# Retention and two gated layers on one core: the second table behind the first keys, side work up to unit 5 in another order, and a limit on the bytes of loads in flight

## The chip, the cores and the metric

One core of one Trainium2 chip runs the kernel. The metric is the device time of one execution in microseconds. The engines are called as in the profile: PE (TensorE matmul), PEld (its weight loads), DVE (VectorE), ACT (ScalarE), POOL (GpSimd) and SP (SyncE, which here only issues transfers). A "q" behind the name of an engine means the sequencer that issues its instructions and transfers.

## What is computed

The reference has three stages; the output of each is the input of the next.

```python
# q, k, v: (2, 8, 768, 64); scale = 1/8
for t in range(S):
    state = gamma * state + einsum('bhd,bhe->bhde', k[:, :, t], v[:, :, t])
    y[:, :, t] = scale * einsum('bhd,bhde->bhe', q[:, :, t], state)
x = y.transpose(0, 2, 1, 3).reshape(1536, 512)
x = (x @ w_a) * (x @ w_b) @ w_out             # 512 -> 1536 -> 512
h = x @ w_in                                  # 512 -> 2048
out = maximum(0.01 * h, h) @ w_out2           # 2048 -> 512
```

`gamma` is one constant for each of the 8 heads. All numbers are float32.

## The kernel before

**Units.** The first stage is cut into 12 units: three tiles of 512 tokens, and in each four pairs of heads. Unit u has four input tiles of 128x512 float32 (256 KB): queries `q`, keys turned `k`, keys plain `n`, values `v`. In the trace all units share these names, so that `q` at one time is the `q` of whichever unit stands there. For each unit the kernel makes scaled keys `kd` and scaled queries `qs`, the scores `sc` (PE), masked scores `P` (DVE), the products of keys and values `kv` (PE), running states (`cb` and `ca` in units 0 to 3, `cr` and `ca` from unit 4 on; DVE), and the output bank `x` (PE), which gets a part from `P` ("within") and a part from the states ("across"). Units 0 to 3 are "wide" (chunks of 128 tokens; their states are copied into the tile `wk` by ACT, `wide_spreads`); units 4 to 11 use chunks of 64 tokens.

**Splitting.** The large products are made of float32 numbers split in two: `x00h` is the high part of the output of tile 0, pair 0 and `x00l` the rest. ACT makes the high part (`x_high`), and the low part is made by DVE (`x_low`), or by POOL from the copy `xf` (`copy_x`). The weights come as raw words (`raw_a`, `raw_b`, 512 KB each), which ACT and DVE round in six steps (`begin_steps` on ACT, tiles `a` and `sl`; `round_steps` on DVE, min, shift and add) before they are split as well (`a0h`, `a0l`).

**Order.** The schedule is written out by hand: each engine executes its instructions in the order of the program, and waits where an operand is not there yet. One loop over u issues for each step the scores and states of unit u + 1 and the output of unit u. From unit 4 on the loop also puts pieces of the first dense layer between (`fill`, generator `first_blocks`): the first piece is the bank `pa`, whose twelve matmuls (L1016) read `x00h`, `x00l`, `x01h`, `x01l`, `x02h`, `x02l`, `x03h`, `x03l` with `a0h`, and then four of them with `a0l`. In the rest of the kernel, two dense layers, PE works through a list of matmuls.

**Transfers.** Two small tables hold constants: `table` (74 KB) is needed for the first scaled queries and keys, `rest` (198 KB) holds among others the causal mask of the first `P`, the rows from which POOL makes `grown`, and the factors of `kd4` and later. ACT issues both. SP issues all inputs, first the four tiles of units 0 to 3, then of unit 4, then `raw_a0`, unit 5, `raw_b0`, unit 6, and so on. Each transfer uses one of eight completion semaphores in turn, so an issue waits until the transfer eight places before it has landed.

**Before the first unit** PE runs ten matmuls on a tile `warm` that DVE has cleared.

Of the kernel before, what the change touches and what calls it, by code (L numbers as in the profile page):

```python
# [9 lines left out]
F32 = mybir.dt.float32  # L10
F32R = mybir.dt.float32r
F16 = mybir.dt.float16
BF16 = mybir.dt.bfloat16
# [7 lines left out]
P = 128  # L21
# [14 lines left out]
NRAW = 4  # L36
NEXTRA = 10
NWARM = 10
FILL = {4: 4, 5: 6, 6: 6, 7: 6, 8: 6, 9: 6, 10: 6, 11: 4}
PUMP = {7: 1.2, 8: 1.6, 9: 1.2, 10: 1.2, 11: 1.2}  # L40
ROUND = {3: ("a", 0, 3), 4: ("b", 0, 3), 5: ("a", 1, 3), 6: ("b", 1, 3)}
# [188 lines left out]
def retention_moe_kernel(ctx: ExitStack, tc: tile.TileContext, ins, out):  # L230
# [11 lines left out]
    def bank(name):  # L242
        return psum.tile([P, TT], F32, tag="ps", name=name)
# [32 lines left out]
    first_layer = len(order)  # L276
    order += second
    source = {"a": (wab, 0), "b": (wab, 1), "wo": (wo, 0), "wi": (w2, 0), "wq": (w2, 1)}
    raws, begun, rounded, dram = {}, {}, {}, {}
    at = {"load": 0, "begin": 0, "round": 0, "queued": 0, "hold": True}  # L280

    def wait_for(later, done):
# [2 lines left out]
            mybir.DependencyInfo(mybir.DependencyClass.Sync, mybir.DependencyReason.DATA),  # L285
        )

    def load_weights(behind=()):
        if at["load"] < len(order) and at["load"] < at["round"] + NRAW:
            kind, f = order[at["load"]]  # L290
            src, i = source[kind]
            t = rawp.tile([P, TT], I64, tag="raw", name=f"raw_{kind}{f}")
            load = nc.sync.dma_start(t, src[f, i])
            if behind:
                wait_for(load, behind[-1])
            raws[kind, f] = t
            at["load"] += 1
# [11 lines left out]
    def begin_steps():  # L309

        n = at["begin"]
        key = order[n]
        raw = raws[key]
        u = slots.new(F32, f"{key[0]}{key[1]}")
        sl = tmp.tile([P, TT], I32, tag="sl", name=f"sl{n}")
        nc.scalar.activation(u, word(raw, F32, 1), AF.Abs, scale=2.0 ** -112)
        yield
        nc.scalar.mul(half(sl, F16, 1), word(raw, F32, 1), 2.0 ** -100)
        yield
        nc.scalar.mul(half(sl, U16, 0), word(raw, U32, 0), 2.0 ** -29)  # L320
        begun[key] = (u, sl)
        at["begin"] += 1
# [191 lines left out]
        return t.rearrange("p (m t) -> p m t", m=SUB)  # L514

    def known(f):
        return lambda u: f(u, *units[u], un[u]) if 0 <= u < len(units) else []

    def loads(u):
        if u >= len(units):  # L520
            return
        d = un[u] = {}
        source = {"q": qT, "k": kT, "n": kn, "v": vn}
        for name in "qknv" if u < NPAIR else "nvqk":
            d[name] = slots.new(F32, f"{name}{u}")
            nc.sync.dma_start(d[name], source[name][units[u]])

    flip = heads[::-1]
    cols = [slice(j * P, (j + 1) * P) for j in range(CPT)]
# [68 lines left out]
        slots.done(1)  # L598

    @known  # L600
    def scaled_keys(u, t, p, d):
        d["kd"] = slots.new(F32, f"kd{u}")
        nc.scalar.activation(d["kd"], d["n"], AF.Copy, scale=small[:, p:p + 1])

    @known
    def scaled_queries(u, t, p, d):
# [71 lines left out]
    @known  # L678
    def masked(u, t, p, d):
        d["P"] = slots.new(F32, f"P{u}")  # L680
        n = 2 * NPAIR + p
        pace[:] = nc.vector.scalar_tensor_tensor(
            by_sub(d["P"]), by_sub(d["sc"]), small[:, n:n + 1], within_sub, op0=ALU.mult, op1=ALU.mult
        ),
# [16 lines left out]
    @known  # L701
    def copy_x(u, n, p, d):
        t = TURN[n]
        if t != 1:
            xf[t, p] = slots.new(F32, f"xf{t}{p}")
            if t:
                nc.scalar.mul(xf[t, p], d["x"], -1.0)
            else:
                nc.scalar.copy(xf[t, p], d["x"])
            if u < NPAIR - 2:  # L710
                nc.gpsimd.tensor_sub(x[t, p][1], xf[t, p], as32(x[t, p][0]))
        slots.done(6)
        del un[u]
# [246 lines left out]
            leave(0, 1, [m], u["p1"], nc.vector.tensor_add, z.acc["p3"])  # L960


    warm = ap.tile([P, TT], BF16, tag="warm", name="warm")
    nc.vector.memset(warm, 0.0)
    nc.scalar.dma_start(table, head)
    loads(0)
    nc.scalar.copy(carry[0][0][:, 0:1], warm[:, 1:2])
    nc.scalar.dma_start(rest, more)
    grow_tables()
    wps = bank("warm")  # L970

    def keep_warm(n):
        for _ in range(n):
            nc.tensor.matmul(wps, warm[:, 0:P], warm, start=True, stop=True)

    keep_warm(NWARM)
    for u in range(1, 4):
# [59 lines left out]
    def keys(u):  # L1037
        (wide_keys if u < NPAIR else scaled_keys)(u)
# [28 lines left out]
    for u in range(-1, len(units)):  # L1067
        if u < NPAIR:
            if u < NPAIR - 1:
                wide_scores(u + 1)  # L1070
            else:
                wide_within(u)
                issue(states(u + 1))
                issue(scores(u + 1))
            if u < 0:
                queries(1)
                keep_warm(3)
            if u < NPAIR - 1:
                wide_states(u + 1)
            else:  # L1080
                un[u + 1]["copy"]()
                for step in un[u + 1]["adds"][:2]:
                    step()
                masked(u + 1)
                for step in un[u + 1]["adds"][2:]:
                    step()
                for _ in rounds:
                    pass
            if u < 0:
                wide_within(0)  # L1090
            if 1 < u < NPAIR - 1:
                wide_within(u)
            wide_across(u)
            if not u:
                wide_within(1)
            if u == NPAIR - 2:
                keys(NPAIR)
                queries(NPAIR)
            x_high(u)
            if u == NPAIR - 2:  # L1100
                begin = begin_steps()
                next(begin)
                wide_spreads(u + 1)
                keys(NPAIR + 1)
                queries(NPAIR + 1)
                for _ in begin:
                    pass
                x_low(u)
                rounds = weigh_steps(u + 1)
                next(rounds)  # L1110
                next(rounds)
                loads(u + AHEAD)
                slots.tick()
                continue
            if u < NPAIR - 1:
                wide_spreads(u + 1)
            if u < 0:
                keys(1)
            for v in KEYS.get(u, ()):
                keys(v)  # L1120
                queries(v)
            if u == NPAIR - 1:
                copy_x(u - 1)
                high(done.pop())
                x_low(u)
                low()
                keys(NPAIR + 2)
                begin_weights()
            copy_x(u)
            slots.tick()  # L1130
        else:
            issue(states(u + 1), within(u))
            issue(scores(u + 1), across(u))
            slots.tick()
            steps = un[u + 1]["adds"] if u + 1 in un else []
            mid = len(steps) // 2
            if steps and u > NPAIR:
                un[u + 1]["copy"]()
            if u == NPAIR:
                masked(u + 1)  # L1140
                un[u + 1]["copy"]()
                for step in steps:
                    step()
                x_high(u)
                queries(u + 2)
                weigh(u)
                high(done.pop())
                x_low(u)
                low()
                begin_weights()  # L1150
            else:
                low()
                for step in steps[:mid]:
                    step()
                masked(u + 1)
                for step in steps[mid:mid + 1]:
                    step()
                keys(u + 2)
                for v in QUERIES.get(u, ()):
                    queries(v)  # L1160
                leave_x(u)
                for step in steps[mid + 1:]:
                    step()
                if u == NPAIR + 1:
                    fill(u)
                rounding(u)
            copy_x(u)
        if u != NPAIR + 1:
            fill(u)
        pump(PUMP.get(u, 0))  # L1170
        loads(u + AHEAD)
        if u < 0:
            load_weights()
        if u in (5, 6, 8, 9, 10, 11):
            load_weights(pace if u > 6 else ())
        if u == 9:
            at["hold"] = False
        if u == 6:
            enqueue_next(2)
            queue.extend(behind)  # L1180
            behind.clear()
            queue.extend(sub_items(("a", 2), ("b", 2)))
        if u == 8:
            for d, a in outer:
                nc.gpsimd.dma_start(xf[d], xf[a], accum_op=ALU.add)
        if u == 8:
            spare.extend(mixed_items(xf, S, "s", True))
        for _ in range(min(LATER.get(u, 0), len(spare))):
            spare.pop(0)[1]()
        slots.tick()  # L1190
# [438 lines left out]
```

## Time and profile before

| | us |
|---|---|
| median of 3 runs | 557.0 (556.24 to 559.15) |
| profiled execution, whole | 557.07 |
| its span, first to last instruction | 555.3 |
| PE busy in the span | 548.9 (99%) |
| DVE busy | 457.5 (82%) |
| ACT busy | 385.8 (69%) |
| POOL busy | 158.9 (29%) |

The table is read from the top: 1.77 us of the profiled execution lie outside the span. PE is busy nearly all the time; matmuls are pipelined and their ends are modelled, so that the idle 6.4 us are not all that PE could save. Nearly all of the trace in which PE is not the engine that sets the pace lies in the first 45 us, in which the inputs are loaded.

### The profile page before, as it was taken

What the parts mean: (1) busy time and instruction counts of PE and PEld (TensorE: products, weight loads), DVE (VectorE), ACT (ScalarE), POOL (GpSimd) and SP (SyncE); (2) the same over time, 40 slices, a digit from 0 to 9 for tenths busy, and PEclk for the clock granted to TensorE, in tenths of its full rate; (3) what the DMA queues carried; (4) which work ended last, traced back from release to release, by engine and by line L of the source; (5) the groups of instructions that cost most, each with busy time, mean ns of one, the idle gap of its engine ahead of it and who ended that gap; (6) DMA issues with size and microseconds to landing.
All of it is one profiled execution on the core that took longest, in us unless ns stands there. A gap on an engine that the chain in (4) does not pass through costs nothing.

```text
span 555.3 us, 10484 instructions
## 1 busy us (share of the span) xinstructions
PE 548.9 (99%) x3743; PEld 462.5 (83%) x3743; DVE 457.5 (82%) x973; ACT 385.8 (69%) x797; POOL 158.9 (29%) x203
## 2 busy tenths in 40 slices
PE   8999999999999999999999999999999999999997
PEld 5878888888888888888888888888888888888886
DVE  4877967889898898899789859896977798999862
ACT  4867377877789888867758457769766886687800
POOL 3524201113231430267520320221433556700000
PEclk9999999999999999999999999999999999999999
DMA  8996934548788987899992362665787799964111
GB/s 313 393 375 167 217 93 119 154 133 212 195 253 219 259 220 253 260 305 240 243 186 94 66 125 71 184 181 158 231 240 233 206 272 242 223 164 118 58 58 57
DMA packets 49765, 108.19 MB, mean 195 GB/s; under 512 B 5936, under 2 KB 13360, under 8 KB 49712
## 3 DMA queue, kind: packets, MB, share of 16 engines
q1 hardware_dynamic: 27360, 66.60, 36.7%
q0 software_dynamic: 22064, 40.64, 34.5%
q8 instruction: 29, 0.48, 0.3%
q10 hardware_dynamic: 288, 0.28, 0.2%
q14 instruction: 24, 0.20, 0.1%
HBM read 73.68 MB, written 18.35 MB: 166 GB/s over the span
## 4 chain that ended last, share of the span: by engine, by line
PE 95%; DMA 3%; DVE 1%; issue 0%; ACT 0%; SPq 0%
PE blk L258 12%; PE blk L257 12%; PE blk L259 12%; PE top L257 6%; PE top L258 5%; PE top L259 5%; PE pa L257 4%; PE pa L259 4%; PE pa L258 4%; PE pb L257 4%; PE pb L259 4%; PE pb L258 4%; PE mid L257 3%; PE mid L259 3%; PE mid L258 3%; DMA q<-in_qT 2%
## 5 line engine op out<-in xcount | busy, mean ns | idle before, releaser
L258 PE MATMUL blk<-form,form 128*128 128x512 f32 (+1 forms) x224 | 75.8, 339 | 0.0
L257 PE MATMUL blk<-form,form 128*128 128x512 f32 (+1 forms) x224 | 75.6, 337 | 0.0
L259 PE MATMUL blk<-form,form 128*128 128x512 f32 (+1 forms) x224 | 75.3, 336 | 0.0
L173 DVE TENSOR_TENSOR form<-g,form 128x512 fp32r<-128x512 f32 x112 | 57.6, 551 | 0.9
L258 PE MATMUL blk<-forma,forma 128*128 128x512 f32 (+1 forms) x168 | 56.9, 338 | 0.0
L257 PE MATMUL blk<-forma,forma 128*128 128x512 f32 (+1 forms) x168 | 56.7, 337 | 0.0
L259 PE MATMUL blk<-forma,forma 128*128 128x512 f32 (+1 forms) x168 | 56.4, 336 | 0.0
L167 ACT CAST form<-g 128x512 fp32r<-128x512 f32 x112 | 52.4, 512 | 4.7 <-DMA g<-g 2.8
L257 PEld LDWEIGHTS blk<-form,form 128*128 128x128 f32 x224 | 42.5, 190 | 5.3
L173 DVE TENSOR_TENSOR forma<-h,forma 128x512 fp32r<-128x512 f32 x84 | 43.0, 551 | 4.5 <-ACT forma L167 3.0
L258 PEld LDWEIGHTS blk<-form,form 128*128 128x128 f32 x224 | 42.5, 190 | 4.7
L259 PEld LDWEIGHTS blk<-form,form 128*128 128x128 f32 x224 | 42.3, 189 | 4.8
L167 ACT CAST forma<-h 128x512 fp32r<-128x512 f32 x84 | 38.8, 511 | 2.8 <-DMA h<-h 2.8
L763 POOL DMA_DIRECT2D farg<-g x26 | 15.6, 616 | 80.7 <-ACT g L1373 62.8
L146 POOL DMA_DIRECT2D h<-h x33 | 33.0, 1133 | 14.3 <-DVE forma L173 3.9
L257 PEld LDWEIGHTS blk<-forma,forma 128*128 128x128 f32 x168 | 31.9, 190 | 3.9
L258 PEld LDWEIGHTS blk<-forma,forma 128*128 128x128 f32 x168 | 31.9, 190 | 3.6
L259 PEld LDWEIGHTS blk<-forma,forma 128*128 128x128 f32 x168 | 31.7, 189 | 3.6
L763 POOL DMA_DIRECT2D farh<-h x19 | 11.0, 576 | 74.6 <-DVE h L893 50.3
L173 DVE TENSOR_TENSOR form<-wq,form 128x256 fp32r<-128x256 f32 x56 | 23.4, 418 | 10.0 <-ACT form L167 9.9
L167 ACT CAST form<-wq 128x256 fp32r<-128x256 f32 x56 | 22.6, 403 | 6.3 <-PE blk L258 2.8
L146 POOL DMA_DIRECT2D g<-farg x22 | 22.0, 1040 | 9.1 <-DVE form L173 5.6
(3062 smaller groups left out, 1680.4 us busy)
## 6 DMA issues: line engine op xcount, KB each, us to landing
raw_wi<-in_w SPq DMA_DIRECT2D x16, 512.0 KB, 4.3
raw_wq<-in_w SPq DMA_DIRECT2D x16, 512.0 KB, 5.0
farg<-g POOLq DMA_DIRECT2D x26, 256.0 KB, 4.5
g<-farg SPq DMA_DIRECT2D x26, 256.0 KB, 6.6
raw_a<-in_wab SPq DMA_DIRECT2D x12, 512.0 KB, 4.5
raw_b<-in_wab SPq DMA_DIRECT2D x12, 512.0 KB, 4.9
raw_wo<-in_wo SPq DMA_DIRECT2D x12, 512.0 KB, 5.0
g<-farg POOLq DMA_DIRECT2D x20, 256.0 KB, 8.8
```

What stands on the lines that cost most here:

```text
L146: queue.append((0.0, lambda piece=piece: self.nc.gpsimd.dma_start(self.A(*d[1:], j)[piece], self.A(*x1[1:], j)[piece], accum_op=ALU.add)))
L167: nc.scalar.copy(h, src)
L173: nc.vector.tensor_sub(*todo.pop(0))
L257: nc.tensor.matmul(ps, w[0], x[0], start=first, stop=False, skip_group_check=more)
L258: nc.tensor.matmul(ps, w[0], x[1], start=False, stop=False, skip_group_check=more)
L259: nc.tensor.matmul(ps, w[1], x[0], start=False, stop=last, skip_group_check=more)
L763: nc.gpsimd.dma_start(self.far[t, f], self.tiles[t, f])
```

## The change

Four things change; the arithmetic is the same except that the matmuls ahead of the first unit multiply ones and not zeros.

1. The table `rest` is issued by SP behind `q0` and `k0`, and no longer by ACT.
2. A list `aloft` of loads in flight, in units of 256 KB (a raw weight counts 2): a load waits for the oldest one in the list as soon as the loads behind that one, itself included, come to `FLYING` = 5 units or more. It stands on all inputs and raw weights.
3. Side work moves: in unit 0 ACT scales the keys of unit 1 (`kd1`) before it copies the states into `wk`; at unit 2 ACT copies the states into `wk` before it begins with `raw_a0`; `kd5` is made by POOL and no longer by ACT; `x02l` is made by POOL from `xf02` and no longer by DVE from the bank; the steps of rounding `a0` on DVE stand between the states and the masked scores of unit 4.
4. The matmuls ahead of the first unit, and one small copy, read constants that are there when the program begins. The tile `warm` and its clearing on DVE are gone.

```diff
+FLYING = 5
...
+    def fly(load, size):
+        aloft.append((load, size))
+        if sum(n for _, n in aloft[1:]) >= FLYING:
+            wait_for(load, aloft.pop(0)[0])
+            while sum(n for _, n in aloft[1:]) >= FLYING:
+                aloft.pop(0)
...
             load = nc.sync.dma_start(t, src[f, i])
+            fly(load, 2)
...
-            nc.sync.dma_start(d[name], source[name][units[u]])
+            fly(nc.sync.dma_start(d[name], source[name][units[u]]), 1)
...
-    def scaled_keys(u, t, p, d):
+    def scaled_keys(u, t, p, d, engine=None):
         d["kd"] = slots.new(F32, f"kd{u}")
-        nc.scalar.activation(d["kd"], d["n"], AF.Copy, scale=small[:, p:p + 1])
+        if engine:
+            engine.tensor_scalar(d["kd"], d["n"], small[:, p:p + 1], None, op0=ALU.mult)
+        else:
+            nc.scalar.activation(d["kd"], d["n"], AF.Copy, scale=small[:, p:p + 1])
...
-            if u < NPAIR - 2:
+            if u < NPAIR - 1:
                 nc.gpsimd.tensor_sub(x[t, p][1], xf[t, p], as32(x[t, p][0]))
...
-    warm = ap.tile([P, TT], BF16, tag="warm", name="warm")
-    nc.vector.memset(warm, 0.0)
     nc.scalar.dma_start(table, head)
-    loads(0)
-    nc.scalar.copy(carry[0][0][:, 0:1], warm[:, 1:2])
-    nc.scalar.dma_start(rest, more)
+    loads(0, "qk")
+    nc.scalar.copy(carry[0][0][:, 0:1], nc.const_aps.tensor(0.0, (P, 1), F32))
+    nc.sync.dma_start(rest, more)
+    loads(0, "nv")
...
-            nc.tensor.matmul(wps, warm[:, 0:P], warm, start=True, stop=True)
+            nc.tensor.matmul(wps, ones[:, 0:P], ones, start=True, stop=True)
...
                 for step in un[u + 1]["adds"][:2]:
                     step()
+                next(rounds)
                 masked(u + 1)
+                next(rounds)
...
             if u == NPAIR - 2:
-                begin = begin_steps()
-                next(begin)
                 wide_spreads(u + 1)
-                keys(NPAIR + 1)
+                begin_weights()
+                scaled_keys(NPAIR + 1, nc.gpsimd)
                 queries(NPAIR + 1)
-                for _ in begin:
-                    pass
-                x_low(u)
                 rounds = weigh_steps(u + 1)
-                next(rounds)
-                next(rounds)
...
+            if u < 0:
+                keys(1)
             if u < NPAIR - 1:
                 wide_spreads(u + 1)
-            if u < 0:
-                keys(1)
```

Three places show how it moves instructions. The first is the beginning of SP's queue; the names in brackets are the completion semaphores waited for, and a name such as `q1` is the `q` of unit 1. Before:

```order
L526 DMA q0_1_98<-in_qT 128x512
L526 DMA k0_2_100<-in_kT 128x512
L526 DMA n0_3_102<-in_kn 128x512
L526 DMA v0_4_104<-in_vn 128x512
L526 DMA q1_5_123<-in_qT 128x512
L526 DMA k1_6_125<-in_kT 128x512
L526 DMA n1_7_127<-in_kn 128x512 [waits DMAHW0_49]
L526 DMA v1_8_129<-in_vn 128x512 [waits DMAHW1_49]
L526 DMA q2_9_131<-in_qT 128x512 [waits DMAHW2_49]
```

And now:

```order
L535 DMA q0_1_96<-in_qT 128x512
L535 DMA k0_2_98<-in_kT 128x512
L978 DMA rest_75<-in_more 128x396
L535 DMA n0_3_102<-in_kn 128x512
L535 DMA v0_4_104<-in_vn 128x512
L535 DMA q1_5_121<-in_qT 128x512
L535 DMA k1_6_123<-in_kT 128x512 [waits DMAHW1_49]
L535 DMA n1_7_125<-in_kn 128x512 [waits DMAHW2_49,DMAHW0_49]
L535 DMA v1_8_127<-in_vn 128x512 [waits DMAHW4_49]
L535 DMA q2_9_129<-in_qT 128x512 [waits DMAHW5_49]
```

`rest` stands third. `k1` now waits for `q0`, `n1` for `k0`, `v1` for `n0`, `q2` for `v0`: each load of an input tile for the one five places before it, where it waited for the transfer eight places before it.

The second place is DVE and POOL from the last wide unit to unit 5. DVE before:

```order
L572 SCALAR_TENSOR_TENSOR ca31_84<-cb1_88,table_74,kv3_369 128x64
L695 TENSOR_TENSOR x02l_66_402<-x2_382,x02h_65_401 128x512
L334 TENSOR_SCALAR a0_67_404<-a0_67_404 128x512
L336 TENSOR_SCALAR a0_67_404<-a0_67_404 128x512
L636 COPY cr0_85<-kv4_435 128x64
L625 SCALAR_TENSOR_TENSOR cr0_85<-ca01_78,rest_75,kv4_435 128x64
L625 SCALAR_TENSOR_TENSOR cr0_85<-cr0_85,rest_75,kv4_435 128x2x64
L682 SCALAR_TENSOR_TENSOR P4_74_470<-sc4_450,rest_75 128x512
L625 SCALAR_TENSOR_TENSOR cr0_85<-cr0_85,rest_75,kv4_435 128x2x64
L625 SCALAR_TENSOR_TENSOR ca00_77<-cr0_85,rest_75,kv4_435 128x64
L338 ISA a0_67_404<-a0_67_404,sl0_405 128x1024
```

DVE now:

```order
L581 SCALAR_TENSOR_TENSOR ca31_84<-cb1_88,table_74,kv3_367 128x64
L648 COPY cr0_85<-kv4_430 128x64
L637 SCALAR_TENSOR_TENSOR cr0_85<-ca01_78,rest_75,kv4_430 128x64
L637 SCALAR_TENSOR_TENSOR cr0_85<-cr0_85,rest_75,kv4_430 128x2x64
L343 TENSOR_SCALAR a0_67_404<-a0_67_404 128x512
L694 SCALAR_TENSOR_TENSOR P4_74_466<-sc4_445,rest_75 128x512
L345 TENSOR_SCALAR a0_67_404<-a0_67_404 128x512
L637 SCALAR_TENSOR_TENSOR cr0_85<-cr0_85,rest_75,kv4_430 128x2x64
L637 SCALAR_TENSOR_TENSOR ca00_77<-cr0_85,rest_75,kv4_430 128x64
L347 ISA a0_67_404<-a0_67_404,sl0_405 128x1024
```

Three state steps have moved ahead of the two steps on `a0`, `P4` stands between these two, and `x02l` is gone. POOL before:

```order
L711 TENSOR_TENSOR x01l_55_340<-xf01_56_344,x01h_54_339 128x512
L608 TENSOR_TENSOR qs4_64_399<-q4_19_151,table_74 128x512
L608 TENSOR_TENSOR qs5_69_411<-q5_23_161,grown_76 128x512
L608 TENSOR_TENSOR qs6_90_581<-q6_27_171,grown_76 128x512
L608 TENSOR_TENSOR qs7_97_682<-q7_39_237,grown_76 128x512
```

POOL now:

```order
L723 TENSOR_TENSOR x01l_55_338<-xf01_56_342,x01h_54_337 128x512
L620 TENSOR_TENSOR qs4_64_397<-q4_19_149,table_74 128x512
L613 TENSOR_SCALAR kd5_68_409<-n5_21_155,rest_75 128x512
L620 TENSOR_TENSOR qs5_69_411<-q5_23_159,grown_76 128x512
L723 TENSOR_TENSOR x02l_66_400<-xf02_77_481,x02h_65_399 128x512
L620 TENSOR_TENSOR qs6_90_579<-q6_27_169,grown_76 128x512
```

`kd5` now stands ahead of `qs5`, and `x02l` ahead of `qs6`.

The third place is ACT in the same stretch. Before:

```order
L690 CAST x02h_65_401<-x2_382 128x512
L316 ACTIVATE a0_67_404<-raw_a0_155 128x512
L582 COPY wk1_90<-cb1_88 64x3x64 x2
L603 ACTIVATE kd5_68_409<-n5_21_157,rest_75 128x512
L318 ACTIVATE sl0_405<-raw_a0_155 128x512
L320 ACTIVATE sl0_405<-raw_a0_155 128x512
L690 CAST x03h_75_481<-x3_426 128x512
L709 COPY xf02_77_484<-x2_382 128x512
L989 CAST a0h_78_486<-a0_67_404 128x512
```

And now:

```order
L702 CAST x02h_65_399<-x2_380 128x512
L591 COPY wk1_90<-cb1_88 64x3x64 x2
L325 ACTIVATE a0_67_404<-raw_a0_153 128x512
L327 ACTIVATE sl0_405<-raw_a0_153 128x512
L329 ACTIVATE sl0_405<-raw_a0_153 128x512
L702 CAST x03h_75_478<-x3_421 128x512
L721 COPY xf02_77_481<-x2_380 128x512
L1000 CAST a0h_78_484<-a0_67_404 128x512
```

The copy into `wk` no longer stands behind the first instruction that reads `raw_a0`, and `kd5` is gone from ACT. From the scaled keys of unit 6 on the order of all engines is the same as before.

## Rows read from the trace of the kernel before

**Rows 1.** The profile's busy time of each engine over the span.

```profile
PE 548.9 (99%) x3743; PEld 462.5 (83%) x3743; DVE 457.5 (82%) x973; ACT 385.8 (69%) x797; POOL 158.9 (29%) x203
```

**Rows 2.** The chain that ended last: start, duration (us), what.

```profile
13.41 6.65 DMA raw_a<-in_wab
...
20.09 0.69 ACT a L316
...
25.08 2.94 PE pa L1016 x12
...
28.62 0.89 issue
...
35.82 0.47 issue
```

**Rows 3.** Busy time by stretch, with granted clock, DMA share and GB/s.

```profile
25.00:30.00 5.00, 4.11 (x76) 3.20 (x74) 4.64 (x12) 4.13 (x8) 1.30 (x1) 1.00 1.05 396
...
45.00:50.00 5.00, 5.00 (x116) 4.11 (x118) 3.11 (x9) 3.88 (x7) 3.37 (x4) 1.00 0.43 74
```

**Rows 4.** SP's issues in order of time.

```profile
0.73 0.39 SPq L526 DMA_DIRECT2D q<-in_qT  x1
...
2.59 0.43 SPq L526 DMA_DIRECT2D q<-in_qT  x1
...
7.88 0.33 SPq L526 DMA_DIRECT2D q<-in_qT  x1
```

**Rows 5.** Transfers of the first 45 us: issuer, number, size, median from issue to landing.

```profile
q8 instruction: 6, 0.10, 0.9%
...
q<-in_qT SPq DMA_DIRECT2D x12, 256.0 KB, 5.9
```

**Rows 6.** Loads of 256 KB in quiet stretches later on, tile wi.

```profile
L454 SPq DMA_DIRECT2D wi<-wi x6: 320/320/372, 272.7 to 290.9; - x6
...
DMA to landing us min/median/max: 2.3/2.9/6.2
```

**Rows 7.** First 14 us in order: PE's first matmuls and POOL's first work on rest.

```profile
1.19 4.45 PE L974 MATMUL warm<-warm 128*128 128x512 bf16 x10 [1.19 <-DVE warm L964]
5.36 0.34 POOL L501 COPY grown<-rest 128x192 f32<-128x192 f32 x1 [3.26 <-DMA rest<-in_more]
5.57 1.21 PE L552 MATMUL sc<-qs,k 64*128 64x128 f32 x16
5.78 1.29 POOL L503 TENSOR_SCALAR grown<-rest 128x64 f32<-128x64 f32 x3
```

**Rows 8.** ACT in order of time, 14 to 25 us.

```profile
14.78 0.91 ACT L539 ACTIVATE kd<-n,table 128x256 f32<-128x256 f32 x2 [0.60 <-DMA n<-in_kn]
...
16.80 0.73 ACT L582 COPY wk<-cb 64x192 f32<-64x192 f32 x2 [0.16 <-DVE cb L572]
17.43 0.57 ACT L709 COPY xf<-x 128x512 f32<-128x512 f32 x1
...
24.26 0.62 ACT L989 CAST a0h<-a 128x512 fp32r<-128x512 f32 x1
```

**Rows 9.** POOL in order of time, 18 to 24 us.

```profile
18.08 1.28 POOL L711 TENSOR_TENSOR x01l<-xf,x01h 128x512 fp32r<-128x512 f32 x1 [0.57 <-ACT xf L709]
19.32 1.27 POOL L608 TENSOR_TENSOR qs<-q,table 128x512 f32<-128x512 f32 x1
22.16 1.28 POOL L608 TENSOR_TENSOR qs<-q,grown 128x512 f32<-128x512 f32 x1 [1.57 <-DMA q<-in_qT]
```

**Rows 10.** DVE in order of time, 19 to 24 us.

```profile
20.80 0.43 DVE L334 TENSOR_SCALAR a<-a 128x512 f32<-128x512 f32 x1 [0.42 <-ACT a L316]
...
22.31 0.75 DVE L682 SCALAR_TENSOR_TENSOR P<-sc,rest 128x512 f32<-128x512 f32 x1
...
23.54 0.68 DVE L338 CUSTOM_DVE_ANT_0 a<-a,sl 128x1024 uint16<-128x1024 uint16 x1
```

**Rows 11.** PE in order of time, 20 to 24 us.

```profile
20.69 1.11 PE L675 MATMUL sc<-qs,k 64*64 64x64 f32 x32
...
23.11 0.27 PE L675 MATMUL x<-P,v 64*64 64x64 f32 x2 [0.25 <-DVE P L682]
23.87 0.27 PE L675 MATMUL sc<-qs,k 64*64 64x64 f32 x2
```

More of the change, by code (lines that the diff above doesn't have):

```diff
@@ L278, in retention_moe_kernel @@
     source = {"a": (wab, 0), "b": (wab, 1), "wo": (wo, 0), "wi": (w2, 0), "wq": (w2, 1)}
-    raws, begun, rounded, dram = {}, {}, {}, {}
+    raws, begun, rounded, dram, aloft = {}, {}, {}, {}, []
     at = {"load": 0, "begin": 0, "round": 0, "queued": 0, "hold": True}
@@ L516, in known, with loads @@
     def known(f):
-        return lambda u: f(u, *units[u], un[u]) if 0 <= u < len(units) else []
-    def loads(u):
+        return lambda u, *more: f(u, *units[u], un[u], *more) if 0 <= u < len(units) else []
+    def loads(u, names=None):
         if u >= len(units):
             return
-        d = un[u] = {}
+        d = un.setdefault(u, {})
         source = {"q": qT, "k": kT, "n": kn, "v": vn}
-        for name in "qknv" if u < NPAIR else "nvqk":
+        for name in names or ("qknv" if u < NPAIR else "nvqk"):
             d[name] = slots.new(F32, f"{name}{u}")
-            nc.sync.dma_start(d[name], source[name][units[u]])
+            fly(nc.sync.dma_start(d[name], source[name][units[u]]), 1)
     flip = heads[::-1]
@@ L960, in finish @@
             leave(0, 1, [m], u["p1"], nc.vector.tensor_add, z.acc["p3"])
-    warm = ap.tile([P, TT], BF16, tag="warm", name="warm")
-    nc.vector.memset(warm, 0.0)
     nc.scalar.dma_start(table, head)
-    loads(0)
-    nc.scalar.copy(carry[0][0][:, 0:1], warm[:, 1:2])
-    nc.scalar.dma_start(rest, more)
+    loads(0, "qk")
+    nc.scalar.copy(carry[0][0][:, 0:1], nc.const_aps.tensor(0.0, (P, 1), F32))
+    nc.sync.dma_start(rest, more)
+    loads(0, "nv")
     grow_tables()
-    wps = bank("warm")
+    wps, ones = bank("warm"), nc.const_aps.tensor(1.0, (P, TT), BF16)
     def keep_warm(n):
         for _ in range(n):
-            nc.tensor.matmul(wps, warm[:, 0:P], warm, start=True, stop=True)
+            nc.tensor.matmul(wps, ones[:, 0:P], ones, start=True, stop=True)
     keep_warm(NWARM)
```

## The prediction

> **What bounds the kernel now.** The busy time by engine comes first: PE works 99% of the span [rows 1]. Then the chain that ended last shows where PE does not set the pace: the chain enters PE for good with the bank `pa` at 25.08 us, and behind that only two pieces are no work, 0.89 us at 28.62 and 0.47 us at 35.82, both "issue", in which PE waits for nothing that the profile shows [rows 2]. The busy time by stretch agrees: PE has 4.11 of 5 us from 25 to 30 us, in which the transfer engines are full (share 1.05, 396 GB/s), and 5.00 of 5 us from 45 to 50 us, where their share has fallen to 0.43 [rows 3]. Every edit of this change acts ahead of that point. So its worth is read at one place, the start of `pa`, and at the two stalls behind it; the dense layers behind follow PE and keep whatever comes out.
>
> **The limit on loads.** `q1` was issued at 2.59 us, and the issue at 7.88 us (`q3`, which waits for the transfer eight places before it) shows that it had landed then: 5.29 us [rows 4]. Eight loads of 262,144 bytes in 5.29 us are 396 GB/s, the rate that the stretches show [rows 3]. So a load takes so long (median 5.9 us [rows 5]) because it stands behind seven others, not because it is slow by itself: in a quiet stretch one of the same size landed in 2.3 us [rows 6]. Five loads at 396 GB/s need 3.31 us. As long as a load alone takes less than that, the engines never run dry and every landing stays where it is; the cost is 0, with 1.0 us of cover for each load. The other bound: if a load went on taking 5.29 us, the rate would fall to five eighths. From the landing of `q1` at 7.88 us to that of `q5` at about 22.14 us (`qs5` starts at 22.16 us and waited for it [rows 9]) are 14.26 us, which would become 22.8 us: 8.6 us lost. I take 0: the quiet loads are the row without a queue, and it lies 1.0 us under the 3.31 us. Behind 45 us the limit stands on raw weights alone, one of which waits for the third before it; PE waits for none of them in the stretch shown [rows 3], and I cost it at 0.
>
> The second table now goes out third on SP. POOL, which had waited for it, read it at 5.36 us, and the mask is needed when the first scores end at 5.57 + 1.21 = 6.78 us [rows 7]. The same bytes go through the same full engines in nearly the same order, so I cost it at nothing; the cover is 1.4 us, and SP's issue of 0.43 us [rows 4] is what later loads would lose without the queue of loads that hides it.
>
> **The start.** PE's first ten matmuls waited until 1.19 us for DVE to clear their tile, and the first scores followed at 5.57 us, as these ended [rows 7]. Constants take that wait away, 0 to 1.19 us; I take 0.4 us, since SP, which waited for nothing, began at 0.73 us [rows 4]. The scaled keys of unit 1 also come sooner. But this does not reach unit 4. ACT stands at 14.78 us for the landing of `n3` (`kd3`, 0.60 us of waiting) and is set anew there; behind it the copy into `wk` at 16.80 us waited 0.16 us for DVE, and then come `xf01` at 17.43 us [rows 8], `x01l` on POOL at 18.08 us, which waited for it, and `qs4` from 19.32 to 20.59 us [rows 9]; `sc4` starts on PE at 20.69 us [rows 11]. This line can gain the 0.16 us and no more: `sc4` starts at 20.53 and ends at 20.53 + 1.11 = 21.64 us.
>
> **DVE in unit 4.** `P4` began at 22.31 us though its scores were there at 20.69 + 1.11 = 21.80 us. It stood behind two steps on `a0`, the first at 20.80 us after waiting for ACT [rows 10], which had begun at 20.09 us as `raw_a0` landed [rows 2], and behind three state steps: 22.31 - 20.80 = 1.51 us for the five. `kv4` stands ahead of `sc4` on PE, so the state steps can now run from 20.53 us, 1.51 - 2 x 0.43 = 0.65 us, and one step on `a0` (0.43 us) behind them, to 21.61 us. That is while `sc4` is on PE, so `P4` starts at about 21.68 us, 0.63 us sooner, and PE's output matmuls of unit 4, which came 0.80 us behind the start of `P4` (23.11 us [rows 11]), at 22.48 us.
>
> **POOL in units 4 and 5.** `qs4` ends at 20.43 us. `n5` is issued next behind `raw_a0`, which landed at 13.41 + 6.65 = 20.06 us [rows 2], and lands one load later: 20.06 + 0.66 = 20.72 us, where 0.66 us is 262,144 bytes at 396 GB/s. `kd5` starts then. Its price on POOL is not in the trace. From below, a copy of 192 columns took 0.34 us; from above, three of the same operation on 64 columns took 1.29 us together, 0.43 us each, which for 512 columns, if all of that went with the columns, is 8 x 0.43 = 3.4 us [rows 7]. I take 1.28 us, the product of two tensors of the same size on the same engine [rows 9], since that reads one operand more. Then `kd5` ends at 22.00 us, `qs5` still waits for `q5` and runs from 22.16 to 23.44 us, as before. PE's matmuls of `kv5` and `x4` take 23.87 - 23.11 = 0.76 us until `sc5` [rows 11]: from 22.48 to 23.24 us. There `sc5` now waits for `qs5`, to about 23.50 us. From `sc5` to `pa` it was 25.08 - 23.87 = 1.21 us, so `pa` could start at 24.71 us.
>
> The Trainium skill, "GPSIMD Engine Reference", section "Elementwise — side-by-side cycle accounting", gives 769 ns for a tight loop over 512 elements. By that, `kd5` would end at 21.49 us, `qs5` would start at 22.16 us all the same, and the sum would not change; the rival on `kd5` below would get no chance. No run here shows it yet.
>
> **The rounding.** `pa` also needs `a0h`. Behind `P4` (0.75 us, to 22.43 us) DVE still has one step on `a0`, 0.43 us, and two state steps, 23.54 - 22.31 - 0.75 = 0.48 us; the last rounding step then starts at 23.36 us instead of 23.54 us [rows 10]. `a0h` came 0.72 us after that start and took 0.62 us [rows 8]: it ends at 24.70 us, with a hand-over `pa` starts at 24.76 us. `x02l` on POOL follows `qs5`, 23.44 + 1.28 = 24.72 us with a wait for `xf02` on ACT at most 0.1 us later; the sixth matmul of `pa` reads it, and twelve take 2.94 us [rows 2], so it is due at 24.76 + 5 x 0.245 = 25.99 us: 1.2 us of cover, and without it each microsecond of delay is one of PE. On DVE it had run in a gap, so leaving gives nothing.
>
> **Sum.** `pa` starts 25.08 - 24.76 = 0.32 us sooner. The profiled execution took 557.07 us (555.3 us of span and 1.77 us around it), 0.07 us over the median of the runs. 557.0 - 0.3 = 556.7 us.
>
> **The rivals.**
> *The two stalls shrink.* PE stood still for 0.89 + 0.47 = 1.36 us only while the transfer engines were full [rows 2, 3], and a queue called instruction moves 6 packets in that stage [rows 5]. If these wait behind the loads in flight, fewer loads make them shorter; at the most 556.7 - 1.4 = 555.3 us. Against it: the engines stay full with five loads, and a stall in a full stage is seen, not its cause. The Trainium skill, "DMA: Bandwidth & Descriptors", section "Queues, rings and completion order", says that each transfer engine goes round between its queues packet by packet. By that rule the depth of SP's queue would not matter to another queue, and this rival would gain nothing, 556.7 us.
>
> *`kd5` is long on POOL* (the slower side). At 3.4 us it ends at 24.12 us. PE has `kv5` ahead of `x4` and stands behind it; `qs5` ends at 25.40 us, `sc5` starts at 25.46 us and `pa` at 26.67 us: 1.6 us late, 558.6 us. It decides from about 1.8 us on, where `qs5` ends later than 23.8 us and `sc5` is no longer sooner than it was. For it: an operation of 64 columns took as long as 0.43 us. Against it: the copy of three times as many took 0.34 us, so most of it does not go with the columns.
>
> *The limit starves the loads* (slower too). At five eighths of the rate 556.7 + 8.6 = 565.3 us; at a tenth less, 14.26 x 0.1 = 1.4 us, 558.1 us. It decides where a load alone takes over 3.31 us in this stage. For it: nothing shows a load of this size alone in the first 45 us. Against it: 2.3 us later on.
>
> *The change does nothing at `pa`*, because landings and not the order hold it: 557.0 us. It is too near to the forecast to be told from it by a time.
>
> **The numbers.** The forecast with the last rival 0.60, the stalls 0.20, `kd5` 0.13, the starved loads 0.07. The range from 555.1 to 558.6 us takes in the stalls and the long `kd5` and leaves out the starved loads beyond a tenth. A difference of 0.5% is 2.8 us, about what can be told from no change. Faster by more needs both stalls gone and 1.1 us beside the 0.3 us: 0.04. Slower by more needs starved loads, or a long `kd5` and loads a tenth slower: 0.06. Within: 0.90.
>
> **What would show it.** In the profile after: loads from issue to landing near 3.3 us at about the same GB/s (limit); `sc4` near 20.5 us; `P4` near 21.7 us; one TENSOR_SCALAR of 512 columns on POOL with its price, ending before `q5` lands; `qs5` ending near 23.4 us with PE waiting for it; `pa` near 24.8 us; and the two stalls with the same 0.9 and 0.5 us. The prediction is wrong if landings move by more than half a microsecond either way, since nearly every wait ahead of `pa` ends in one.

## The result, and the profile after

The change makes the kernel slower: 562.9 us (median of 6 runs, 559.9 to 564.8) against 557.0 us before (6 runs, 556.2 to 559.2), a ratio of 1.0099 with a 95% interval from 1.0080 to 1.0118. The forecast was 556.7 us with a range up to 558.6 us; it was wrong. The profiled execution of after is its shortest, 559.92 us, with a span of 558.2 us. It shows 2.9 us of the loss; the median execution lost 3 us more, of which no trace of this kernel shows the whole.

The stretches that answer to [rows 3], and the whole loading stage (10 to 35 us): clock, share of the transfer engines and GB/s stand last. First the loading stage before:

```profile
10.00:35.00 25.00, 23.44 (x515) 20.28 (x512) 19.70 (x48) 21.43 (x43) 10.21 (x8) 1.00 1.05 393
```

And after:

```profile
10.00:35.00 25.00, 21.91 (x497) 18.69 (x496) 18.35 (x40) 16.88 (x34) 12.59 (x9) 1.00 0.93 308
25.00:30.00 5.00, 4.46 (x130) 3.86 (x131) 4.11 (x10) 2.60 (x5) 3.32 (x2) 1.00 0.89 264
45.00:50.00 5.00, 5.00 (x101) 4.17 (x92) 4.17 (x10) 2.21 (x4) 1.36 (x2) 1.00 0.89 279
```

In the 25 us of the loading stage the rate is 308 GB/s, where before it was 393. From 45 to 50 us the kernel before moved 74 GB/s, since its last input had landed at 43.5 us; the changed kernel still moves 279, and its last input lands at 51.3 us. The input tiles of the first 45 us (answers to [rows 5]):

```profile
n<-in_kn SPq DMA_DIRECT2D x12, 256.0 KB, 4.3
q<-in_qT SPq DMA_DIRECT2D x11, 256.0 KB, 4.4
k<-in_kT SPq DMA_DIRECT2D x11, 256.0 KB, 4.5
v<-in_vn SPq DMA_DIRECT2D x11, 256.0 KB, 4.0
```

A load lands 4.0 to 4.5 us after its issue and not 3.3 us as forecast. The order of time on PE, POOL, DVE and ACT around `pa`, which answers to [rows 8 to 11]:

```profile
21.38 0.67 ACT L325 ACTIVATE a<-raw_a 128x512 f32<-128x512 f32 x1 [0.54 <-DMA raw_a<-in_wab]
...
21.64 1.15 PE L687 MATMUL sc<-qs,k 64*64 64x64 f32 x32 [0.36 <-POOL qs L620]
...
22.83 0.75 DVE L694 SCALAR_TENSOR_TENSOR P<-sc,rest 128x512 f32<-128x512 f32 x1 [0.33 <-PE sc L687]
...
23.36 1.56 POOL L613 TENSOR_SCALAR kd<-n,rest 128x512 f32<-128x512 f32 x1 [1.78 <-DMA n<-in_kn]
...
24.81 0.68 DVE L347 CUSTOM_DVE_ANT_0 a<-a,sl 128x1024 uint16<-128x1024 uint16 x1
24.89 1.74 POOL L620 TENSOR_TENSOR qs<-q,grown 128x512 f32<-128x512 f32 x1
24.98 0.27 PE L687 MATMUL kv<-v,kd 64*64 64x64 f32 x2 [1.39 <-POOL kd L613]
...
25.53 0.62 ACT L1000 CAST a0h<-a 128x512 fp32r<-128x512 f32 x1 [0.82 <-DVE a L347]
...
26.59 1.73 POOL L723 TENSOR_TENSOR x02l<-xf,x02h 128x512 fp32r<-128x512 f32 x1
26.68 0.27 PE L687 MATMUL sc<-qs,k 64*64 64x64 f32 x2 [0.55 <-POOL qs L620]
...
27.76 0.50 PE L1027 MATMUL pa<-x00h,a0h 128*128 128x512 f32 x1
```

`pa` starts 2.7 us later than in [rows 2], and the row that decides is `kd5` on POOL: it stood 1.78 us for the landing of `n5` and began at 23.36 us, where the forecast had 20.72 us. `kv5`, `qs5`, `sc5` and `pa` follow in a row. On this way `qs5` took 1.74 us, 0.46 us more than in [rows 9]; it began beside a rounding step of DVE (more on this below). `a0h` ended at 26.15 us and held nobody.

The start went as forecast: PE's first matmuls begin at 0.77 us ([rows 7]: 1.19) and POOL's first read of `rest` is a little sooner.

```profile
0.77 4.42 PE L985 MATMUL warm<-const-bfloat16-1.0 128*128 128x512 bf16 x10 [0.77 <-PEq L1625]
...
5.13 1.25 PE L561 MATMUL sc<-qs,k 64*128 64x128 f32 x16
5.14 0.34 POOL L510 COPY grown<-rest 128x192 f32<-128x192 f32 x1 [3.05 <-DMA rest<-in_more]
```

### The profile page after: what moved, and what is told of

Same layout as the page of the kernel before. It is cut to its first block, busy times and chain, and to the rows that moved or that the text cites. A ratio compares the mean times of both kernels' runs of the same rounds, so it can differ in the third digit from the quotient of the medians.

```text
span 558.2 us, 10492 instructions
## 1 busy us (share of the span) xinstructions
PE 551.0 (99%) x3743; PEld 462.9 (83%) x3743; DVE 459.3 (82%) x971; ACT 385.8 (69%) x796; POOL 162.0 (29%) x205
## 4 chain that ended last, share of the span: by engine, by line
PE 87%; DMA 8%; DVE 2%; ACT 1%; issue 1%; SPq 1%; DVEq 0%; ACTq 0%
PE blk L259 12%; PE blk L258 12%; PE blk L260 12%; PE top L258 6%; PE top L259 5%; PE top L260 5%; DMA k<-in_kT 5%; PE pb L258 3%; PE pb L259 3%; PE pb L260 3%; PE pa L259 3%; PE pa L260 3%; PE pa L258 3%; PE mid L258 3%; PE mid L259 3%; PE mid L260 3%
## 5 line engine op out<-in xcount | busy, mean ns | idle before, releaser
L168 ACT CAST forma<-wo 128x256 fp32r<-128x256 f32 x42 | 16.9, 402 | 12.7 <-PE blk L260 12.7
```

Of the source, the lines that this page charges most:

```text
L168: nc.scalar.copy(h, src)
```

## The experiments

The theory after this result: five loads in flight do not keep the transfer engines full, and this is the whole loss. The rivals: `kd5` on POOL, or another piece of the new order, costs it.

**The change without its limit, and the limit without the rest.** The first sets one number; the second puts the list `aloft` of the change, and nothing else of it, into the kernel before.

```diff
-FLYING = 5
+FLYING = 99
```

> The changed kernel with FLYING = 99, so that no load waits for the limit and all other edits stay. Theory A (the limit alone costs the time): GB/s from 10 to 25 us back at about 390, the bank pa starts near 24.8 us, 556 to 557.2 us, ratio to before 0.998 to 1.001. Theory B (the other order of side work costs it, with kd5, qs5 and x02l in a row on POOL): POOL still holds up PE at kv5 and sc5, at least 559 us, ratio 1.004 or more. If both cost, 558 us.

> The kernel before with the limit alone (FLYING = 5), order and tables as before. Theory A: ratio near 1.010, about 562 us, with 300 to 330 GB/s from 10 to 25 us and 4.3 us from issue to landing of an input tile. Theory B: 557 us, ratio 1.000 to 1.002.

Without the limit: 556.9 us (11 runs), ratio 1.0007 [0.9998, 1.0015]. The limit alone: 563.2 us (5 runs), ratio 1.0112 [1.0094, 1.0130]. The limit is the whole loss, and what the other three parts are worth together cannot be told from nothing. In the profile of the limit alone the rate from 10 to 35 us is 295 GB/s, `pa` starts at 28.4 us, and one sees further places at which the limit costs, 30 and 60 us behind `pa`:

```profile
54.68 0.66 ACT L325 ACTIVATE a<-raw_a 128x512 f32<-128x512 f32 x1 [2.62 <-DMA raw_a<-in_wab]
...
55.38 0.43 DVE L343 TENSOR_SCALAR a<-a 128x512 f32<-128x512 f32 x1 [2.60 <-ACT a L325]
...
58.33 0.69 ACT L612 ACTIVATE kd<-n,rest 128x512 f32<-128x512 f32 x1
...
59.08 0.27 PE L684 MATMUL kv<-v,kd 64*64 64x64 f32 x2 [1.40 <-ACT kd L612]
...
87.20 0.50 PE L258 MATMUL top<-s20h,tb2h 128*128 128x512 f32 x1 [1.60 <-ACT h L912]
```

The third raw weight `raw_a2` is issued at 49.45 us (before: 39.79 us). ACT waits 2.62 us for it, with the scaled keys of a later unit queued behind, and PE waits 1.40 us for these; DVE waits 2.60 us in its turn. PE pays again at 87 us, in the next layer, and this comes by another way, which the chain that ended last shows:

```profile
52.93 0.53 POOL qs L617
...
54.15 0.78 POOL xf L1194
...
73.47 7.79 DMA xf<-xf
...
81.34 0.10 ACT s41h L815
...
86.72 0.43 ACT h L912
```

POOL issues eight transfers `xf<-xf`, each of which adds one tile to another. The first of them stands in POOL's order behind `qs`, which had waited for the last `q` (landed at 52.77 us; before: 42.88 us). The last of them lands at 81.26 us, ACT waits 2.64 us for it with `s41h`, and `h`, for which PE waits 1.60 us, is queued behind that. In the kernel before, the first transfer goes out 7.7 us sooner, and ACT waits neither for a raw weight nor for these transfers:

```profile
46.43 1.94 POOL L1185 DMA_DIRECT2D xf<-xf  x2
...
47.08 0.68 ACT L316 ACTIVATE a<-raw_a 128x512 f32<-128x512 f32 x1
...
71.82 0.62 ACT L806 CAST s41h<-xf 128x512 fp32r<-128x512 f32 x1
```

The transfers also took longer, 6.3 us in the median from issue to landing against 4.3 us before; what lengthened them was not tried. In the changed kernel's own trace ACT waits 1.23 us for `raw_a2` and 1.14 us for the last `xf<-xf`.

**How many loads in flight it takes.** The changed kernel with other numbers for `FLYING`.

> The changed kernel with FLYING = 1: each load waits for the one before it, so that from issue to landing it takes what it takes alone in this stage. The prediction's assumption (a load alone lands in about 2.3 us): median 2.3 to 2.5 us, and the 3.3 us of five at the full rate was within reach. Theory A1 (a load alone in this stage takes longer, 3 us or more): median 3.0 to 4.3 us, so that five cannot fill the engines. The whole gets far slower in either case, 600 us or more.

> The changed kernel with FLYING = 7. Theory A: a smaller part of the loss, 350 to 385 GB/s from 10 to 25 us, 557 to 559.5 us. Theory B: no change against FLYING = 5, about 562 us.

> The changed kernel with FLYING = 3 in place of 5. The profiles so far give, from issue to landing, 2.6 us for a load alone, 4.3 us for five in flight, 5.1 for seven and 5.9 for eight. Theory K (each load in flight adds about 0.4 us to the time of all, with no knee): 2.6 + 2 x 0.4 = 3.4 us, so 3 x 262,144 bytes in 3.4 us, some 230 GB/s from 10 to 20 us, and a time between 563 and 670 us, I expect 575 to 590 us. Rival H (a hard knee: a load keeps its 2.6 us until the engines are full): 2.6 to 2.7 us, 290 to 300 GB/s, the rate of the changed kernel, and its time of 560 to 565 us.

> The changed kernel with FLYING = 6. Theory K: 2.6 + 5 x 0.4 = 4.6 to 4.7 us from issue to landing, about 335 GB/s from 10 to 35 us, and a time between that with 7 (557.3 us) and that with 5 (562.9 us): 558 to 561 us, ratio 1.002 to 1.007. Rival (a step at one number: from six on nothing is lost): 365 GB/s or more and 556.8 to 557.5 us.

| `FLYING` | us from issue to landing (medians of q, k, n, v, 2 to 40 us) | GB/s, 10 to 35 us | time, us |
|---|---|---|---|
| 1 | 2.6 | 106 | 670.0 (1 run) |
| 3 | 3.0 to 3.5 | 235 | 575.2 (1 run) |
| 5 | 4.0 to 4.5 | 308 | 562.9 |
| 6 | 4.8 to 4.9 | 331 | 558.1, ratio 1.0032 [1.0018, 1.0045] |
| 7 | 4.8 to 5.3 | 365 | 557.3, ratio 1.0009 [0.9999, 1.0019] |
| 99 | 6.0 to 6.1 | 390 | 556.9, ratio 1.0007 [0.9998, 1.0015] |

The two rows that decide, 10 to 35 us with one load and with three (PE's granted clock is 0.61 and 0.86 in them, so that these two times hold more than the waiting for loads):

```profile
10.00:35.00 25.00, 12.06 (x136) 10.68 (x136) 6.62 (x17) 3.69 (x10) 1.26 (x1) 0.61 0.37 106
```

```profile
10.00:35.00 25.00, 18.51 (x360) 16.34 (x361) 14.02 (x34) 12.04 (x26) 10.89 (x8) 0.86 0.74 235
```

A load alone takes 2.6 us. This is near the prediction's 2.3 us and under the 3 us of theory A1: a slow lone load is not the reason. With a hard knee three would take 2.6 us too and give 3 x 262,144 bytes / 2.6 us = 302 GB/s; they take about 3.3 us and give 235. On the average each load added makes all of them some 0.4 us slower: (3.3 - 2.6) / 2 = 0.35 us from one to three, (4.3 - 2.6) / 4 = 0.43 us from one to five. The rate bends slowly towards 390 GB/s and is not there at five, six or seven. Nor is time lost between a landing and the next issue: rate times landing time is about as many loads as the limit allows (235 GB/s x 3.3 us = 3.0 loads, 308 x 4.3 = 5.1, 365 x 5.0 = 7.0). What makes the landings longer no run shows. The Trainium skill, "SBUF — State Buffer", section "The DMA setup-cost knee", gives about 2 us plus the bytes at 436 GB/s for a transfer, by which 2.6 us is the estimate for this size; the trace agrees for one load. Of several in flight that section says nothing, and the runs show that its 2 us are not simply overlapped.

**Where the limit costs.** It was put on the loads behind unit 5 alone (`LIMITED = 25, 1000`), and on the first 25 loads alone (`LIMITED = 0, 25`):

```diff
+        limited.append(load)
         if sum(n for _, n in aloft[1:]) >= FLYING:
-            wait_for(load, aloft.pop(0)[0])
+            first = aloft.pop(0)[0]
+            if LIMITED[0] < len(limited) <= LIMITED[1]:
+                wait_for(load, first)
```

> The changed kernel with the limit on raw_b0 and the loads behind it alone (unit 6 on); the loads up to unit 5 go out as before. Theory A (late loads cost twice: once ahead of pa, and again where raw_a2 lands late and ACT and DVE stand before it in unit 8): pa as without limit, about 26.3 us, raw_a2 issued at 43 to 46 us instead of 38 to 40 us, and still 558 to 560.5 us. Rival (only what stands ahead of pa counts): 556.5 to 557.2 us.

> The changed kernel with the limit on the loads up to unit 5 alone; from raw_b0 on they go out as before. Theory A: pa late as in the changed kernel (27.3 to 28 us) but raw_a2 issued by about 42 us, so that the second wait is gone: 557.5 to 559.5 us, clearly under the changed kernel. Rival (only what stands ahead of pa counts): the whole loss, 561.5 to 563 us.

Behind unit 5: 560.8 us (6 runs, 556.7 to 563.5), ratio 1.0075 [1.0053, 1.0097]. Up to unit 5: 559.7 us (5 runs), ratio 1.0049 [1.0037, 1.0062]. So it costs in both halves: 0.0075 + 0.0049 = 0.0124, against 0.0099 for the whole change and 0.0112 for the limit alone. The two are not pieces of the whole cut apart: in the trace of the second kernel `n5` lands at 25.2 us and `pa` starts at 30.4 us, against 23.3 and 27.8 us in the changed kernel and 27.3 to 28 us as expected, and it has no wait of ACT for `raw_a2` or for `xf<-xf`. In the second kernel `kd5` waits 2.64 us for `n5`, PE stands for 2.56 us, and the granted clock then falls to 0.50, the lower of its two levels (1.2 GHz), for the next 3 us:

```profile
24.00:27.00 3.00, 0.63 (x12) 0.38 (x8) 1.71 (x5) 2.44 (x5) 1.74 (x1) 0.95 0.93 285
27.00:30.00 3.00, 2.81 (x104) 2.81 (x108) 2.92 (x4) 1.46 (x3) 3.00 (x3) 0.50 1.05 397
```

In the stretches of after shown above the granted clock is 1.00, so this was no part of the 2.9 us seen there. But over the whole traced execution of this second kernel the mean granted clock is 0.997, and so it is in two of the six executions of after, the longest (563.5 and 564.8 us), where the others have 0.999 or 1.000. The same may have happened in them; no trace of one was taken.

**Longer executions of these kernels.** The profiled execution of the limit behind unit 5 happened to be its shortest (556.69 us), and showed little. The changed kernel was run once more for its trace, and this one twice.

> The changed kernel once more, for a second trace. Theory A: its time follows the landing of the loads: if it is over 561 us, raw_a2 is read by ACT later than the 52.5 us of the first trace, with the difference in the time of about the same size or more; if it is near 560 us, the trace looks like the first.

> The kernel with the limit from raw_b0 on alone, run again for a trace of one of its longer executions (it took 556.7 to 563.5 us). Theory L (the late landing of raw_a2 holds ACT, then DVE, then PE): pa starts at 26 to 27 us as before, raw_a2 is issued behind 46 us where the time is over 559 us, ACT waits over 1 us for it, and PE waits for the a that comes of it. Rival M (what is lost lies ahead of pa, or in the second half): pa behind 27.5 us, or no wait for raw_a2 in a long execution.

> The same kernel a third time, for the same reason: if one of the two executions is short (under 558 us) and one long, their traces should differ in the landing of raw_a2 (theory L) and agree at pa within 0.5 us; under rival M they differ at pa.

The changed kernel took 560.65 us, with `pa` at 28.19 us and ACT waiting 1.7 us for `raw_a2`. The two others took 559.94 and 559.95 us. Of the second, rows of PE and ACT:

```profile
26.48 0.50 PE L1031 MATMUL pa<-x00h,a0h 128*128 128x512 f32 x1 [1.37 <-ACT a0h L1004]
...
51.44 0.67 ACT L329 ACTIVATE a<-raw_a 128x512 f32<-128x512 f32 x1 [2.00 <-DMA raw_a<-in_wab]
...
55.83 0.27 PE L691 MATMUL kv<-v,kd 64*64 64x64 f32 x2 [0.40 <-ACT kd L619]
...
77.15 0.62 ACT L822 CAST s41h<-xf 128x512 fp32r<-128x512 f32 x1 [2.72 <-DMA xf<-xf]
...
83.02 0.50 PE L259 MATMUL top<-s20h,tb2h 128*128 128x512 f32 x1 [0.71 <-ACT h L919]
```

`pa` lies between 25.75 and 26.48 us in all three executions, short and long. ACT waits 2.0 us for `raw_a2` in both long ones and 0.7 us in the short one (issued at 45.63 and 46.09 against 44.60 us). Laid side by side, PE's matmuls of the second long one are 0.7 us behind the short one at `pb` (31 us), 1.5 us at 57 us, 1.9 us at 75 us, 2.9 us at 83 us, and 3.3 us from 97 us on; the span differs by 558.2 - 554.9 = 3.3 us.

The late weight is one piece of this, the step from 0.8 to 1.5 us at 55 to 57 us. The 0.7 us at `pb` come before `raw_a2` is issued. The 1.0 us at 80 us are the other way seen above: POOL's first `xf<-xf` goes out at 50.85 us (47.86 in the short one), the last lands at 77.07 us (72.83), and ACT waits 2.72 us for it (0.76). In the first long one ACT waits 1.61 us there and PE does not stand for it; it loses 1.1 us at 106 us instead, where DVE has waited 3.04 us for another transfer that POOL issues (`a4l`). The smaller steps were not followed up. Why the landings of one kernel differ by over 1 us from execution to execution was not tried and stays open; with it stays open the longest part of the scatter (up to 564.8 us).

**Is anything to be had from the order?** No limit, and both rounding steps of `a0` ahead of `P4`, with `x02l` back on DVE (against the kernel without the limit):

```diff
-            if u < NPAIR - 1:
+            if u < NPAIR - 2:
...
                 next(rounds)
-                masked(u + 1)
                 next(rounds)
+                masked(u + 1)
...
                 queries(NPAIR + 1)
+                x_low(u)
```

> No limit, both rounding steps of a0 on DVE ahead of P4 and x02l back on DVE, so that no rounding step runs while POOL works on qs5 or x02l. Theory P (a rounding step on DVE that meets a product of two tiles on POOL waits for its end: 1.48 us instead of 0.43, 1.19 instead of 0.68): both steps near 0.43 to 0.7 us, the last one 0.68 us, a0h ends by 25.2 us and PE does not wait for it at pa. Then theory F (PE also cannot go on before its instructions have come, the 0.9 and 0.5 us that the profile calls issue): these stalls are back, and the time stays within 0.1% of the kernel without limit, about 556.8 us. Against F: 1.2 us less, 555.7 us.

556.8 us (11 runs), ratio 1.0002 [0.9992, 1.0012]. `pa` comes 0.8 us sooner than without the limit alone (25.53 against 26.33 us), and the first stall is back. Not all went as expected: the last rounding step still met `qs5` and took 1.24 us and not 0.68, so that `a0h` ended at 25.48 us and not by 25.2 us. The chain of this kernel:

```profile
21.20 1.85 POOL kd L613
...
25.53 3.06 PE pa L1027 x12
...
29.14 0.94 issue
...
31.71 2.94 PE pb L1027 x12
```

`pb` starts at 31.71 us; without the limit alone, where the chain holds only 0.08 us of "issue" behind `pa`, it started at 31.40 us. What PE gains at `pa` it stands for a few microseconds later. The traced execution (557.9 us) is over the median. It has one more stall of PE that nothing in the profile explains, 0.64 us at 46.62 us, which no other trace here has. No kernel tried beats the one before.

## Why the prediction was wrong

**The step that failed is the cost of the limit, "I take 0".** It took the transfer engines as a server that is full as long as five loads alone would fill it ("As long as a load alone takes less than that, the engines never run dry", 2.6 us against 3.31 us). The load alone took 2.6 us, under the 3.31 us asked for, and the engines still ran below their rate, 308 of 393 GB/s: with five in flight each load took 4.3 us. The rival *the limit starves the loads* was what happened, but its own point of decision was wrong in the same way, and so was its chance of 0.07. Its formula with the measured rates gives 14.26 x (393 / 308 - 1) = 3.9 us; `q5` landed 2.5 us later than before, and `pa` lost 2.7 us. (At a rate a tenth lower it gives 14.26 / 0.9 - 14.26 = 1.6 us, and not the 1.4 us of the prediction.) The quiet row was also misread. [rows 6] takes in two kinds of transfers of `wi`, and the 2.3 us belong to those that POOL issues to store a tile:

```profile
L345 POOL DMA_DIRECT2D wi<-wi x6: 539/560/624, 130.1 to 198.8; - x6
...
DMA to landing us min/median/max: 2.3/2.4/5.2
```

SP's six loads by themselves took longer:

```profile
DMA to landing us min/median/max: 2.7/5.9/6.2
```

So the cover was at best 3.31 - 2.7 = 0.6 us and not 1.0. That the measured 2.6 us still lies under 3.31 us did not save the step.

**The second failed step is "Behind 45 us ... I cost it at 0".** It read PE alone in a stretch of before, in which loading had ended. At the lower rate loading goes on, `raw_a2` is issued 5 to 10 us later, and ACT, which has other work queued behind the reading instruction, waits for it. The last `q` lands later too, and with it POOL's transfers behind it start later. The limit behind unit 5 costs 0.75% by itself. A slower stream is paid at each place where its cover ends, and the bound of 8.6 us asked about one only.

**The order edits** can be judged in the kernel without the limit, whose loads run at 390 GB/s. Rows of PE, DVE and POOL:

```profile
20.54 1.10 PE L687 MATMUL sc<-qs,k 64*64 64x64 f32 x32
...
20.85 1.56 POOL L613 TENSOR_SCALAR kd<-n,rest 128x512 f32<-128x512 f32 x1 [0.40 <-DMA n<-in_kn]
...
21.80 0.74 DVE L694 SCALAR_TENSOR_TENSOR P<-sc,rest 128x512 f32<-128x512 f32 x1
...
22.38 1.28 POOL L620 TENSOR_TENSOR qs<-q,grown 128x512 f32<-128x512 f32 x1
...
22.47 1.48 DVE L345 TENSOR_SCALAR a<-a 128x512 int32<-128x512 int32 x1
...
23.65 1.42 POOL L723 TENSOR_TENSOR x02l<-xf,x02h 128x512 fp32r<-128x512 f32 x1
...
24.44 1.19 DVE L347 CUSTOM_DVE_ANT_0 a<-a,sl 128x1024 uint16<-128x1024 uint16 x1
...
26.33 0.50 PE L1027 MATMUL pa<-x00h,a0h 128*128 128x512 f32 x1 [1.38 <-ACT a0h L1000]
```

| | forecast | without the limit |
|---|---|---|
| `sc4` starts | 20.53 | 20.54 |
| `P4` starts | 21.68 | 21.80 |
| `kd5` starts, lasts | 20.72, 1.28 | 20.85, 1.56 |
| `qs5` ends | 23.44 | 23.66 |
| `a0h` ends | 24.70 | 26.28 |
| `pa` starts | 24.76 | 26.33 |

The start, DVE's and POOL's steps were right within 0.3 us, apart from the rounding, and in this trace the rival of a long `kd5` fell: 1.56 us is under the 1.8 us from which it decides. In eleven traces `kd5` took from 1.56 to 1.87 us, and in the kernel with the steps ahead, at 1.84 us from 21.20 us on, it does stand in the chain before `pa`. (1.56 us is twice the 769 ns that the Trainium skill, "GPSIMD Engine Reference", section "Elementwise — side-by-side cycle accounting", gives for a tight loop; the measurement decides.)

**The rounding was mis-sized.** It priced DVE's steps as in [rows 10], 0.43 and 0.68 us, where POOL was idle or just done. Now they fall on `qs5` and `x02l` and take 1.48 and 1.19 us, 1.05 + 0.51 = 1.56 us more; `a0h` is 1.58 us late. (The prediction's own terms start the last step at 22.43 + 0.43 + 0.48 = 23.34 us and not at 23.36; nothing hangs on that.) Each ends shortly behind POOL's instruction (23.95 behind 23.66 us, 25.63 behind 25.07 us), as if it had stood for it, while `P`, read from a bank, kept its 0.74 us beside POOL.

The other traces bear this out: in ten of them the last step began while POOL worked on `qs5` or `x02l`, and in all ten it ended 0.54 to 0.55 us behind POOL, whether it took 1.11 or 1.76 us. Where it began before POOL's instruction, as in after, it took its 0.68 us and POOL's was the longer one, `qs5` with 1.74 us. The Trainium skill, "SBUF — State Buffer", section "Who interferes with whom", says that DVE shares a pair of ports with POOL, and that it is an exclusive lock for some of DVE's instructions; the rows with `qs5` and `x02l` agree. Beside `kd5` not every row does: in after, DVE's second step began 0.14 us into `kd5`, took 0.82 us and ended 0.60 us before it. The cause itself was not tried by a run of its own.

**The two stalls** went away, yet not as that rival had it: without the limit they are gone as well (0.08 us), and in the kernel with `pa` at 25.53 us the first is back without any limit. In the traces it stands where `pa` starts at 25.08 or 25.53 us and in none where `pa` starts at 25.75 us or later. So it comes where PE reaches this stretch early, and the 1.25 us by which `pa` is later without the limit than before left the time as it was. What ends such a stall the profile does not name, and whether the depth of SP's queue has a part in it no run here decides.

## What to carry to other kernels

A load's time alone says when one load lands, not how many keep the engines full: read the rate at two depths of queue, or expect a limit to cost rate long before it falls to what the lone load suggests. When a stream of loads gets slower, go through all of its readers to the last load, and look at what is queued behind each, transfers of other engines too. And before moving steps between DVE and POOL, lay their instructions side by side in time: a price read where the other engine was idle does not hold beside it.

## What was not expected of the hardware

With 256 KB loads from one queue, 5 in flight gave 308 GB/s, 6 gave 331, 7 gave 365 and the full eight 390, while a load alone took 2.6 us. With a limit of five on all loads or on a part of them, single executions of one kernel scattered by up to 6.8 us (556.7 to 563.5 us), against 3 us before. DVE's last rounding step, begun beside a product of two tiles on POOL, ended 0.54 to 0.55 us behind POOL in each of ten traces.
